# Layer norm of the first tiles by ACT's square root, their transposes inside V, and SwiGLU units ordered by weight columns

## The chip, the cores and the metric

The kernel runs on one core of a Trainium2 chip. Its engines are named as the profile names them: PE (TensorE), DVE (VectorE), ACT (ScalarE), POOL (GpSimd) and SP (SyncE, which here only issues DMAs). The metric is the device time of one execution in microseconds; the median of several runs is compared.

## The reference

One layer norm feeds two branches, linear attention with a Hedgehog feature map and a SwiGLU block, and both are added to the input. All inputs and the output are bfloat16; S = 2048 tokens, D = 640, H = 32 heads of 20, F = 1536.

```python
xn = layernorm(A_x)                       # over the 640 features, eps 1e-5
q, k, v = split(xn @ wqkv)                # (B, H, S, 20) each
pq, pk = q @ w_phi, k @ w_phi             # per head, 20 x 20
phi_q = concat(softmax(pq), softmax(-pq)) # 40 features per head; phi_k likewise
kv = einsum("bhsf,bhsd->bhfd", phi_k, v)
z = einsum("bhsf->bhf", phi_k)
o = einsum("bhqf,bhfd->bhqd", phi_q, kv) / (einsum("bhqf,bhf->bhq", phi_q, z) + 1e-6)
A = o.reshape(B, S, D) @ wo
B = (silu(xn @ w1) * (xn @ w3)) @ w2
out = x + A + B
```

## The kernel before

**Tiles.** The tokens are cut into 16 tiles of 128 (`NST`), and for the SwiGLU products into 4 groups of 512 (`NSC`). D is five chunks of 128 (`KD`), F twelve (`KF`). Each tile is loaded in its natural layout into `xin` (which lies inside `reg_h`), normalised in place, and transposed into `xnT`, whose columns are tokens. Tiles 0 to 3 are transposed by PE through the PSUM tile `pst` and copied out by ACT; tiles 4 to 15 by DMA transposes that SP issues (`x_transposed`, written `T(t)` in the schedule).

**Layer norm.** `ln_stats(t)` is two `bn_stats` and a `bn_aggr` on DVE, which leave mean and variance in `mv`. `ln_pow` is two operations on POOL: the variance plus epsilon (`ve`), and its power of -0.5 (`ry`). `ln_newton` refines that by one Newton step: on DVE for tiles 0 to 3 (two operations, which leave -2 times the value, and ACT multiplies by -0.5 as it copies the transposes out), on POOL for the rest. `ln_x` normalises the tile, on DVE, or on ACT for tiles 12 and 13 (`BY_ACT`).

**Stages.** The work is written out by hand, engine queue by engine queue, and every engine runs its instructions in that order. In the V stage, `V(t)` (`v_unit`, ten matmuls through `by_token`, and two copies by ACT into `vaug`) alternates with `unit()`, one SwiGLU unit. A unit (`glu_unit`) takes 128 columns of w1 and of w3 against 512 tokens: five matmuls for `gp`, five for `up`, a tanh on ACT, and, when the returned function is called (`g0()` and so on), two DVE products into `hT`. `glu` is the list of the 48 units in their order, one token group after the other. Five of them run in the V stage. `FB(d)` (`fuse`) then multiplies w_phi into the k weights, `wkphi`. The phi loop over 16 tiles computes the features of k (`pk`), the sums `kv`, and 31 units; a last loop of 20 turns computes the features of q (`pq`), in its first four turns three units each, from the fifth on the output of one tile per turn (`out_unit`, PSUM tile `acc`).

**PSUM.** Six banks rotate for `pst`, `pv`, `gp`, `up`, `pk`, `pq`, `pf` and `acc`: a matmul into a bank waits until the earlier tile in it has been read.

**Loads.** All DMAs are issued by SP, in order. Two small ACT copies of one element, made after the inverse roots of tile 0 and of tile 1, hold back the loads of tiles 4 and on and of the first SwiGLU weight columns (`ld_glu`). The SwiGLU weights come by columns: 0 to 256 and 256 to 512 early, 512 to 768 in the V stage behind T(9), 768 to 1536 behind it.

```python
T, V = x_transposed, v_unit
...
stats(0, 1)
nc.scalar.copy(out=xin[0:1, 1, 0, 0:1], in_=ry[0:1, 0:1])
ld_tiles(4, 2)
...
lx(0, 1); T(0); warm(4); lx(1, 1); T(1)
V(0); V(1)
stats(2, 1); stats(3, 1)
lx(2, 1); T(2); lx(3, 1); T(3)
...
V(2); V(3)
```

`warm` issues matmuls on zeros, 48 of them before the first transpose.

Of the kernel before, what the change touches and what calls it, by code (L numbers as in the profile page):

```python
# [8 lines left out]
P = 128  # L9
# [3 lines left out]
def kernel(  # L13
# [94 lines left out]
    def ld(dst, src):  # L108
        nc.sync.dma_start(out=dst, in_=src)
# [4 lines left out]
    def ld_glu(f0, f1):  # L114
        for w, src in ((w1, B_w1), (w3, B_w3)):
            ld(w[:, :, f0:f1], src[:, f0:f1].rearrange("(c p) f -> p c f", p=P))

    wps = one.tile([P, KD, Dh], bf, name="wps")
    with tc.manual_schedule():
        def ldT(dst, i, d):  # L120
            rows = slice(d * P, (d + 1) * P)
            nc.sync.dma_start_transpose(
                out=dst[:, :, rows], in_=A_wqkv[rows, i * D : (i + 1) * D]
            )
# [22 lines left out]
        make_identity(nc, ident[:])  # L147
        mhalf = one.tile([P, 4], f32, name="mhalf")
        nc.gpsimd.memset(mhalf[:], -0.5)

        mask = one.tile([P, KD, 8], bf, name="mask")
        nc.gpsimd.memset(mask[:], 1.0)
# [34 lines left out]
        for w in (wkphi, wqphi):  # L187
            nc.gpsimd.memset(w[:, 0, D:FW], 0.0)

        nc.scalar.activation(  # L190
            out=vaug[:, :, :, 20].rearrange("p t h -> p (t h)"),
            in_=ident[:, 0:1].to_broadcast([P, NST * H]), func=AF.Copy, scale=0.0, bias=1.0,
        )


        mv = one.tile([P, NST, 2], f32, name="mv")
        rstd = one.tile([P, NST], f32, name="rstd")

        def ln_stats(t):
            xt = xin[:, (t // 4) % 3, t % 4, :]  # L200
            st = work.tile([P, 2, 6], f32, name="st")
            for i in range(2):
                nc.vector.bn_stats(out=st[:, i, :], in_=xt[:, i * HD : (i + 1) * HD])  # L203
            nc.vector.bn_aggr(out=mv[:, t, :], in_=st[:])  # L204

        ry = one.tile([P, NST], f32, name="ry")
# [3 lines left out]
        def ln_pow(t, n):  # L210
# [3 lines left out]
            )  # L214
            nc.gpsimd.tensor_tensor(out=ry[:, r], in0=ve[:, r], in1=mhalf[:, 0:n], op=ALU.pow)  # L215

        def ln_newton(t, n):


            r = slice(t, t + n)  # L220
            eng = nc.vector if t < BY_DMA else nc.gpsimd
            if n == 1:
                eng.tensor_scalar(
                    out=rstd[:, r], in0=ry[:, r], scalar1=ve[:, r], scalar2=ry[:, r],
                    op0=ALU.mult, op1=ALU.mult,
                )
# [3 lines left out]
            if t < BY_DMA:  # L230
                nc.vector.scalar_tensor_tensor(
                    out=rstd[:, r], in0=rstd[:, r], scalar=-3.0, in1=ry[:, r],
                    op0=ALU.add, op1=ALU.mult,
                )
            else:
                nc.gpsimd.tensor_scalar(
                    out=rstd[:, r], in0=rstd[:, r], scalar1=-0.5, scalar2=1.5,
                    op0=ALU.mult, op1=ALU.add,
                )
                nc.gpsimd.tensor_mul(out=rstd[:, r], in0=rstd[:, r], in1=ry[:, r])  # L240
            if t in BY_ACT:
                nc.gpsimd.tensor_scalar(
                    out=shift[:, r], in0=mv[:, r, 0], scalar1=rstd[:, r], scalar2=-1.0,
                    op0=ALU.mult, op1=ALU.mult,
                )
# [11 lines left out]
                op0=ALU.subtract, op1=ALU.mult,  # L257
            )

        def x_transposed(*ts):  # L260

            for t in ts:
                xn = xin[:, (t // 4) % 3, t % 4, :]
                if t >= BY_DMA:
                    nc.sync.dma_start_transpose(out=xnT[:, :, t * P : (t + 1) * P], in_=xn)
                    continue
                ps = bank("pst", bf)
                for c in range(KD):
                    nc.tensor.transpose(
                        ps[:, c * P : (c + 1) * P], xn[:, c * P : (c + 1) * P], ident[:]  # L270
                    )

                for c0, c1 in ((0, 2), (2, KD)):
                    nc.scalar.mul(
                        out=xnT[:, c0:c1, t * P : (t + 1) * P],
                        in_=ps[:, c0 * P : c1 * P].rearrange("p (c s) -> p c s", s=P),
                        mul=-0.5,
                    )

        def tile_of(t):  # L280
            return slice(t * P, (t + 1) * P)

        def by_token(cols, w, name, cut):


            ps = [bank(name), bank(name)]
            for c in range(KD):
                for i in range(2):
                    a, b = (0, cut) if i == 0 else (cut, w.shape[2] if c == 0 else D)
                    nc.tensor.matmul(  # L290
                        ps[i][:, 0 : b - a],
                        xnT[:, c, cols],
                        w[:, c, a:b],
                        start=(c == 0),
                        stop=(c == KD - 1),
                        skip_group_check=True,
                    )
            return ps

        def v_unit(t, cols=None):  # L300
            ps = by_token(cols or tile_of(t), wv, "pv", HD)
# [252 lines left out]
            )  # L554


        glu = [(sc, fi) for sc in range(NSC) for fi in range(KF)]

        def fill(n):
            for _ in range(n):  # L560
# [2 lines left out]
        def stats(t0, n):  # L563
            for t in range(t0, t0 + n):
                ln_stats(t)
            ln_pow(t0, n)
            if t0 >= BY_DMA:
                ln_newton(t0, n)

        def lx(t0, n):  # L570
            if t0 < BY_DMA:
                ln_newton(t0, n)
            for t in range(t0, t0 + n):
                ln_x(t)

# [12 lines left out]
        def unit():  # L588
            return glu_unit(*glu.pop(0))


        stats(0, 1)
        nc.scalar.copy(out=xin[0:1, 1, 0, 0:1], in_=ry[0:1, 0:1])
        ld_tiles(4, 2)
        ld_tiles(6, 2)
        stats(1, 1)
        nc.scalar.copy(out=w1[0:1, 0, 0:1], in_=ry[0:1, 1:2])
        ld_glu(0, 256)
        ld_tiles(8, 2)
        ld_tiles(10, 2)  # L600
# [75 lines left out]
        for t in range(NST):  # L676
# [7 lines left out]
            fill(1)  # L684
            if t >= 12:
                norm_unit(wkphi, 0, t - 12)
        ld(wo, A_wo.rearrange("(c p) d -> p c d", p=P))

        for t in range(NST + 4):
            if t < NST:
                phi_unit(t, wqphi, "pq")
            if t < 2:
                kv_unit(NST - 2 + t, acc, False, t == 1)
                if t == 1:
                    kv_done(acc)
                    for k in range(0, KF, 4):
                        ld(
                            w2[:, k : k + 4],  # L700
                            B_w2[k * P : (k + 4) * P, :].rearrange("(c p) d -> p c d", p=P),
                        )
# [78 lines left out]
```

## Time and profile before

| | |
|---|---|
| three timed runs | 272.3, 272.51, 273.26 us (median 272.51) |
| profiled execution | 272.0 us, of which the span of the core's instructions is 270.3 us |
| instructions | 5192 |
| busy, share of the span | PE 98%, PE weight loads 61%, DVE 70%, ACT 41%, POOL 36% |
| moved by DMA | 27.80 MB, mean 103 GB/s |
| granted TensorE clock | 1.00 |

Times in the profile are microseconds from the start of the span. A row of a timeline gives start, duration, engine, source line, operation, what it writes and reads with the shapes, and how many instructions the row stands for; in brackets follow the idle time of the engine before it and what ended that. Rows of the groups give busy time and mean nanoseconds of one instead. `reg_h`, `reg_v` and `reg_w` are regions that hold several tiles in turn: an SP row that writes `reg_h` from `in_A_x` is a load of x, one that writes `reg_w` from `in_A_wqkv` a load of attention weights, one that writes `w` a load of SwiGLU weights, and `xnT<-reg_h` a DMA transpose.

### The profile page before, as it was taken

How to read it: one execution, taken by the hardware profiler on the slowest of the kernel's cores; microseconds unless marked ns; L12 is line 12 of the kernel's file. 1: busy time of each engine (PE TensorE's matmuls, PEld its weight loads, DVE VectorE, ACT ScalarE, POOL GpSimd, SP SyncE). 2: the span in 40 equal slices, each digit the busy share in tenths (PEclk: the TensorE clock that was granted, in tenths of full speed). 3: DMA queues.
4: the chain of work that ended last, by engine and by line, in shares of the span. 5: the costliest groups of instructions: out<-in, count | busy, mean ns of one | idle time of the engine just before them, and what ended most of it. 6: DMA issues, size and time to landing. Idle time of an engine off the chain costs nothing.

```text
span 270.3 us, 5192 instructions
## 1 busy us (share of the span) xinstructions
PE 263.7 (98%) x1990; PEld 165.9 (61%) x1990; DVE 189.8 (70%) x349; ACT 109.6 (41%) x258; POOL 97.1 (36%) x104
## 2 busy tenths in 40 slices
PE   7899999999999999999999999999999999999995
PEld 6646576555555555555555455677777777777773
DVE  5999921986677777787768788876766777776341
ACT  6734578344555544455663545422222222221000
POOL 6254720643333333444333321333334444433000
PEclk9999999999999999999999999999999999999999
DMA  7996958940000000000001934346766665576931
GB/s 219 310 246 129 180 117 248 190 122 2 0 0 2 0 2 0 0 5 0 0 2 24 300 75 86 77 109 144 139 136 134 145 130 126 126 144 136 150 101 55
DMA packets 64380, 27.80 MB, mean 103 GB/s; under 512 B 50144, under 2 KB 64352, under 8 KB 64352
## 3 DMA queue, kind: packets, MB, share of 16 engines
q1 hardware_dynamic: 64352, 27.43, 44.9%
q8 instruction: 17, 0.28, 0.4%
q14 instruction: 11, 0.09, 0.1%
HBM read 12.81 MB, written 2.62 MB: 57 GB/s over the span
## 4 chain that ended last, share of the span: by engine, by line
PE 87%; DVE 5%; POOL 3%; DMA 3%; issue 1%; ACT 0%; DVEq 0%
PE acc L505 27%; PE gp L387 17%; PE up L387 17%; PE pq L290 8%; PE pk L290 8%; PE pv L290 4%; DVE st L203 2%; PE pkv L413 2%; PE pr L442 2%; DMA xnT<-reg_h 2%; POOL ry L215 1%; PE pf L371 1%; DVE reg_h L255 1%; DMA reg_h<-in_A_x_dram 1%; DVE mv L204 1%
## 5 line engine op out<-in xcount | busy, mean ns | idle before, releaser
L353 POOL TENSOR_TENSOR phi<-phi,rk 128x1320 bf16<-128x1320 bf16 x32 | 77.2, 2412 | 136.2 <-DVE rk L352 128.4
L350 DVE TENSOR_REDUCE sk<-phi 128x66 f32<-128x1320 bf16 x32 | 48.9, 1529 | 41.2 <-ACT phi L317 40.2
L387 PEld LDWEIGHTS <-w 128*128 128x128 bf16 x480 | 45.5, 97 | 50.7 <-DMA w<-in_B_w_dram 0.3
L387 PE MATMUL up<-xnT,w 128*128 128x512 bf16 x240 | 59.6, 379 | 0.0
L387 PE MATMUL gp<-xnT,w 128*128 128x512 bf16 x240 | 59.6, 379 | 0.0
L290 PEld LDWEIGHTS <-xnT 128*128 128x128 bf16 x480 | 45.5, 97 | 21.7 <-DMA xnT<-reg_h 1.3
L505 PE MATMUL acc<-reg_v,reg_h 128*128 128x320 bf16 (+2 forms) x384 | 54.9, 299 | 0.0
L317 ACT ACTIVATE phi<-pq 128x360 bf16<-128x360 f32 (+1 forms) x64 | 23.3, 451 | 59.2 <-POOL phi L353 53.8
L505 PEld LDWEIGHTS <-reg_h 128*128 128x128 bf16 x384 | 37.3, 98 | 14.5
L395 ACT ACTIVATE th<-gp 128x512 f32<-128x512 f32 x48 | 28.8, 600 | 34.5 <-PE gp L387 30.9
L403 DVE SCALAR_TENSOR_TENSOR reg_h<-gs,up 128x512 bf16<-128x512 bf16 x48 | 33.0, 688 | 5.3 <-PE up L387 0.5
L317 ACT ACTIVATE phi<-pk 128x360 bf16<-128x360 f32 (+1 forms) x64 | 23.3, 451 | 24.5 <-PE pk L290 15.5
L400 DVE SCALAR_TENSOR_TENSOR gs<-th,gp 128x512 bf16<-128x512 f32 x48 | 31.6, 659 | 0.0
L514 DVE TENSOR_TENSOR res<-acc,xr 128x320 bf16<-128x320 f32 (+2 forms) x32 | 14.3, 486 | 21.5 <-PE acc L505 21.5
L290 PE MATMUL pk<-wkphi,xnT 128*128 128x360 bf16 (+2 forms) x160 | 24.7, 300 | 0.0
L290 PE MATMUL pq<-wqphi,xnT 128*128 128x360 bf16 (+2 forms) x160 | 24.6, 300 | 0.0
L505 PE MATMUL acc<-reg_w,reg_v 128*128 128x320 bf16 (+2 forms) x160 | 24.5, 299 | 0.0
L290 PE MATMUL pv<-reg_w,xnT 128*128 128x320 bf16 x160 | 23.0, 299 | 0.5 <-DMA xnT<-reg_h 0.5
L352 DVE RECIPROCAL rk<-sk 128x66 f32<-128x66 f32 x32 | 18.1, 566 | 3.2
L505 PEld LDWEIGHTS <-reg_v 128*128 128x128 bf16 x160 | 15.6, 98 | 6.1
L303 ACT CAST reg_v<-pv 128x320 bf16<-128x320 f32 x32 | 12.1, 430 | 9.7 <-PE pv L290 9.7
L203 DVE BATCH_NORM_STATS2 st<-reg_h 128x6 f32<-128x320 bf16 x32 | 13.6, 467 | 2.1 <-DMA reg_h<-in_A_x_dram 2.1
(62 smaller groups left out, 134.3 us busy)
## 6 DMA issues: line engine op xcount, KB each, us to landing
xr<-in_A_x_dram SPq DMA_DIRECT2D x16, 160.0 KB, 2.5
out_dram<-res SPq DMA_DIRECT2D x15, 160.0 KB, 1.8
reg_h<-in_A_x_dram SPq DMA_DIRECT2D x7, 320.0 KB, 4.9
w<-in_B_w_dram SPq DMA_DIRECT2D x6, 320.0 KB, 5.8
w<-in_B_w_dram SPq DMA_DIRECT2D x2, 960.0 KB, 6.7
reg_v<-in_B_w_dram SPq DMA_DIRECT2D x3, 640.0 KB, 5.9
reg_w<-in_A_wo_dram SPq DMA_DIRECT2D x1, 800.0 KB, 5.3
reg_w<-in_A_wqkv_dram SPq DMA_DIRECT2D x2, 320.0 KB, 4.0
```

The source lines that it names most:

```text
L203: nc.vector.bn_stats(out=st[:, i, :], in_=xt[:, i * HD : (i + 1) * HD])
L290: nc.tensor.matmul(ps[i][:, 0 : b - a], xnT[:, c, cols], w[:, c, a:b], start=(c == 0), stop=(c == KD - 1), skip_group_check=True,)
L317: nc.scalar.activation(out=to[g], in_=p.rearrange("p (c f) -> p c f", f=60), func=AF.Exp, scale=1.0 - 2.0 * g,)
L350: nc.vector.reduce_sum(out=sk[:], in_=rows, axis=AX.X)
L352: nc.vector.reciprocal(out=rk[:], in_=sk[:])
L353: nc.gpsimd.tensor_mul(out=rows, in0=rows, in1=rk[:, :, :, None].to_broadcast([P, 2 * NCH, 3, Dh]))
L387: nc.tensor.matmul(ps[:], w[:, c, fi * P : (fi + 1) * P], xnT[:, c, sc * 512 : (sc + 1) * 512], start=(c == 0), stop=(c == KD - 1),)
L395: nc.scalar.activation(out=th[:], in_=gp[:], func=AF.Tanh, scale=0.5)
L400: nc.vector.scalar_tensor_tensor(out=gs[:], in0=th[:], scalar=1.0, in1=gp[:], op0=ALU.add, op1=ALU.mult)
L403: nc.vector.scalar_tensor_tensor(out=hT[:, 4 * sc : 4 * sc + 4, fi, :], in0=gs[:].rearrange("p (t s) -> p t s", t=4), scalar=0.5, in1=up[: ...
L505: nc.tensor.matmul(ps[:, 0 : b - a], rows[j][0], rows[j][1][:, a:b], start=(j == 0), stop=(j == len(rows) - 1),)
L514: nc.vector.tensor_tensor(out=res[:, a:b], in0=ps[:, 0 : b - a], in1=xr[:, a:b], op=ALU.add)
```

## The change

Tiles 0 to 3 get their inverse root in two steps without POOL: a square root on ACT (`ln_root`, epsilon added as the bias) and a reciprocal on DVE, in place of two POOL operations and two DVE ones. ACT loads the square root's table at the start, and the table for tanh and exp after V(2)'s copies, each by a one-element activation into `table`. The copies that hold loads back move from ACT to POOL. ACT's fill of the ones in `vaug` covers eight tiles instead of sixteen, POOL fills the others.

The transposes of tiles 2 and 3 move into V(1) and V(2), after three of the five chunks, with tile 3's root between the two copies of tile 2's transposes, and tile 2's normalisation between the two halves of tile 3's statistics. ACT copies the transposes without a factor.

The list `glu` is ordered by weight columns: the first four chunks (512 columns) for all four token groups, then the other eight. Six units run in the V stage, the last loop starts with two units instead of three in its first turn. The columns from 512 on are loaded in one piece, behind T(15) and a weight transpose; the load behind T(9) is gone. wo is loaded in two pieces instead of one, w2 in four instead of three.

```diff
+        table = one.tile([P, 1], f32, name="table")
+        nc.scalar.activation(out=table[:], in_=nought[:, 0:1], func=AF.Sqrt)
         nc.scalar.activation(
-            out=vaug[:, :, :, 20].rearrange("p t h -> p (t h)"),
-            in_=ident[:, 0:1].to_broadcast([P, NST * H]), func=AF.Copy, scale=0.0, bias=1.0,
+            out=vaug[:, 0:8, :, 20].rearrange("p t h -> p (t h)"),
+            in_=nought[:, 0:1].to_broadcast([P, 8 * H]), func=AF.Identity, bias=1.0,
         )
+        nc.gpsimd.memset(vaug[:, 8:NST, :, 20], 1.0)
...
-        def ln_stats(t):
+        def ln_stats(t, between=None):
...
             for i in range(2):
                 nc.vector.bn_stats(out=st[:, i, :], in_=xt[:, i * HD : (i + 1) * HD])
+                if i == 0 and between:
+                    between()
...
+        def ln_root(t):
+            r = slice(t, t + 1)
+            nc.scalar.activation(
+                out=ry[:, r], in_=mv[:, t, 1:2], func=AF.Sqrt, bias=eps[:, 0:1], scale=1.0
+            )
...
-        def x_transposed(*ts):
+        def x_transposed(*ts, between=None):
...
                 for c0, c1 in ((0, 2), (2, KD)):
-                    nc.scalar.mul(
+                    nc.scalar.copy(
                         out=xnT[:, c0:c1, t * P : (t + 1) * P],
                         in_=ps[:, c0 * P : c1 * P].rearrange("p (c s) -> p c s", s=P),
-                        mul=-0.5,
                     )
+                    if c0 == 0 and between:
+                        between()
...
-        def by_token(cols, w, name, cut):
+        def by_token(cols, w, name, cut, between=(KD, None)):
             ps = [bank(name), bank(name)]
             for c in range(KD):
+                if c == between[0]:
+                    between[1]()
...
-        glu = [(sc, fi) for sc in range(NSC) for fi in range(KF)]
+        glu = [
+            (sc, fi) for cols in (range(0, 4), range(4, KF)) for sc in range(NSC) for fi in cols
+        ]
...
         def lx(t0, n):
             if t0 < BY_DMA:
-                ln_newton(t0, n)
+                nc.vector.reciprocal(out=rstd[:, t0 : t0 + n], in_=ry[:, t0 : t0 + n])
...
-        stats(0, 1)
-        nc.scalar.copy(out=xin[0:1, 1, 0, 0:1], in_=ry[0:1, 0:1])
+        ln_stats(0)
+        ln_root(0)
+        nc.gpsimd.tensor_copy(out=xin[0:1, 1, 0, 0:1], in_=ry[0:1, 0:1])
...
         lx(1, 1)
         T(1)
+        ln_stats(2)
+        ln_root(2)
         V(0)
-        V(1)
-        stats(2, 1)
-        stats(3, 1)
-        lx(2, 1)
-        T(2)
+        def third():
+            T(2, between=lambda: ln_root(3))
+        ln_stats(3, between=lambda: lx(2, 1))
+        V(1, between=(3, third))
         lx(3, 1)
-        T(3)
+        V(2, between=(3, lambda: T(3)))
+        nc.scalar.activation(out=table[:], in_=nought[:, 0:1], func=AF.Tanh)
...
-        V(2)
         V(3)
...
         g2 = unit()
         g1()
+        lx(8, 1)
+        T(8)
+        g3 = unit()
+        g2()
+        lx(9, 1)
+        T(9)
+        ldT(wkT, 1, 2)
         V(4)
         V(5)
-        g2()
+        stats(10, 2)
+        g3()
         V(6)
-        lx(8, 1)
-        T(8)
-        lx(9, 1)
-        T(9)
-        ld_glu(512, 768)
-        ldT(wkT, 1, 2)
         V(7)
-        stats(10, 2)
-        g3 = unit()
         stats(12, 1)
-        stats(13, 1)
+        g4 = unit()
         lx(10, 2)
         T(10, 11)
+        stats(13, 1)
         V(8)
-        g3()
+        g4()
         stats(14, 2)
         lx(12, 1)
         T(12)
         V(9)
-        g4 = unit()
+        g5 = unit()
         lx(13, 1)
         T(13)
         ldT(wkT, 1, 3)
         V(10)
         phi_blocks()
-        g4()
+        g5()
         lx(14, 2)
         T(14, 15)
         ldT(wkT, 1, 4)
         V(11)
-        ld_glu(768, F)
+        ld_glu(512, F)
...
             if t < 4:
-                fill(3)
+                fill(3 if t else 2)
```

More of the change, by code (lines that the diff above doesn't have):

```diff
@@ L149 @@
         nc.gpsimd.memset(mhalf[:], -0.5)
+        eps = one.tile([P, 1], f32, name="eps")
+        nc.gpsimd.memset(eps[:], EPS)
         mask = one.tile([P, KD, 8], bf, name="mask")
@@ L215, in ln_pow @@
             nc.gpsimd.tensor_tensor(out=ry[:, r], in0=ve[:, r], in1=mhalf[:, 0:n], op=ALU.pow)
+        def ln_root(t):
[3 more added lines that the diff above has]
+            )
         def ln_newton(t, n):
             r = slice(t, t + n)
-            eng = nc.vector if t < BY_DMA else nc.gpsimd
+            eng = nc.gpsimd
             if n == 1:
@@ L229, in ln_newton @@
                 eng.tensor_mul(out=rstd[:, r], in0=rstd[:, r], in1=ve[:, r])
[L230 to L240, printed above, removed]
+            eng.tensor_scalar(
+                out=rstd[:, r], in0=rstd[:, r], scalar1=-0.5, scalar2=1.5,
+                op0=ALU.mult, op1=ALU.add,
+            )
+            eng.tensor_mul(out=rstd[:, r], in0=rstd[:, r], in1=ry[:, r])
             if t in BY_ACT:
-                nc.gpsimd.tensor_scalar(
+                eng.tensor_scalar(
                     out=shift[:, r], in0=mv[:, r, 0], scalar1=rstd[:, r], scalar2=-1.0,
@@ L298, in by_token, with v_unit @@
             return ps
-        def v_unit(t, cols=None):
-            ps = by_token(cols or tile_of(t), wv, "pv", HD)
+        def v_unit(t, cols=None, between=(KD, None)):
+            ps = by_token(cols or tile_of(t), wv, "pv", HD, between)
             for i in range(2):
@@ L566, in stats @@
             ln_pow(t0, n)
-            if t0 >= BY_DMA:
-                ln_newton(t0, n)
+            ln_newton(t0, n)
         def lx(t0, n):
             if t0 < BY_DMA:
-                ln_newton(t0, n)
+                nc.vector.reciprocal(out=rstd[:, t0 : t0 + n], in_=ry[:, t0 : t0 + n])
             for t in range(t0, t0 + n):
@@ L589, in unit @@
             return glu_unit(*glu.pop(0))
-        stats(0, 1)
-        nc.scalar.copy(out=xin[0:1, 1, 0, 0:1], in_=ry[0:1, 0:1])
+        ln_stats(0)
+        ln_root(0)
+        nc.gpsimd.tensor_copy(out=xin[0:1, 1, 0, 0:1], in_=ry[0:1, 0:1])
         ld_tiles(4, 2)
         ld_tiles(6, 2)
-        stats(1, 1)
-        nc.scalar.copy(out=w1[0:1, 0, 0:1], in_=ry[0:1, 1:2])
+        ln_stats(1)
+        ln_root(1)
+        nc.gpsimd.tensor_copy(out=w1[0:1, 0, 0:1], in_=ry[0:1, 1:2])
         ld_glu(0, 256)
@@ L686 @@
                 norm_unit(wkphi, 0, t - 12)
-        ld(wo, A_wo.rearrange("(c p) d -> p c d", p=P))
+        for c0, c1 in ((0, 3), (3, KD)):
+            src = A_wo[c0 * P : c1 * P, :]
+            ld(wo[:, c0:c1], src.rearrange("(c p) d -> p c d", p=P))
         for t in range(NST + 4):
@@ L697 @@
                     kv_done(acc)
-                    for k in range(0, KF, 4):
+                    for k in range(0, KF, 3):
                         ld(
-                            w2[:, k : k + 4],
-                            B_w2[k * P : (k + 4) * P, :].rearrange("(c p) d -> p c d", p=P),
+                            w2[:, k : k + 3],
+                            B_w2[k * P : (k + 3) * P, :].rearrange("(c p) d -> p c d", p=P),
                         )
             if t < 4:
-                fill(3)
+                fill(3 if t else 2)
             else:
```

## The prediction

> **What bounds the kernel now.** I read the page's shares first, then busy time by stage, TensorE's waits, and the timelines of the stage in which TensorE waits. The stages:
>
> ```profile
> span 270.3 us, 5192 instructions
> PE 263.7 (98%) x1990; PEld 165.9 (61%) x1990; DVE 189.8 (70%) x349; ACT 109.6 (41%) x258; POOL 97.1 (36%) x104
> ...
> 14.30:20.70 6.40, 6.40 (x31) 2.79 (x30) 5.91 (x16) 2.55 (x5) 3.42 (x14) 1.00 1.13 231
> 20.70:26.10 5.40, 5.40 (x41) 3.91 (x41) 5.04 (x13) 2.27 (x6) 2.33 (x8) 1.00 0.64 124
> 26.10:33.80 7.70, 7.25 (x42) 3.83 (x40) 7.19 (x19) 4.42 (x10) 5.97 (x19) 1.00 1.01 177
> ...
> 43.70:267.10 223.40, 223.40 (x1679) 138.56 (x1676) 158.80 (x266) 83.51 (x201) 77.18 (x32) 1.00 0.38 86
> ```
>
> The columns after the stretch are its length, then busy time of PE, weight loads, DVE, ACT, POOL, then the granted clock (full everywhere). From 43.7 to 267.1 us PE is never free. A change in the first 43.7 us therefore moves the end one for one, and it can win only time in which PE waits there. The timeline of PE and the queue of SP, which issues the DMAs:
>
> ```profile
> 6.21 0.45 PE L269 MATMUL pst<-ident,reg_h 128*128 128x128 bf16 x5 [0.95 <-POOL ry L215]
> 7.23 0.45 PE L269 MATMUL pst<-ident,reg_h 128*128 128x128 bf16 x5 [0.34 <-DVE reg_h L255]
> 7.52 2.88 PE L290 MATMUL pv<-reg_w,xnT 128*128 128x320 bf16 x20
> 11.24 0.45 PE L269 MATMUL pst<-ident,reg_h 128*128 128x128 bf16 x5 [0.56 <-DVE reg_h L255]
> 14.25 1.24 PE L387 MATMUL gp<-xnT,w 128*128 128x512 bf16 x5
> 18.56 1.24 PE L387 MATMUL gp<-xnT,w 128*128 128x512 bf16 x5
> 33.82 4.25 PE L290 MATMUL pv<-reg_w,xnT 128*128 128x320 bf16 x30 [0.47 <-DMA xnT<-reg_h]
> 43.56 1.65 PE L290 MATMUL pk<-wkphi,xnT 128*128 128x360 bf16 x10
> 26.39 1.14 SPq L109 DMA_DIRECT2D w<-in_B_w_dram  x2
> 28.90 6.89 SPq L265 DMA_TRANSPOSE xnT<-reg_h  x4
> 28.90 4.87 DMA xnT<-reg_h
> 38.70 1.36 PE pv L290 x10
> ```
>
> Two losses are to be seen. The first SwiGLU unit starts only at 14.25, because the transposes of tiles 0 to 3 wait for the layer norm on DVE and POOL. And V(10) at 33.82 waits for the DMA transpose of tile 10, issued at 28.90 and 4.87 us under way behind two weight loads of 26.39. The last two rows are from the chain of waits. A SwiGLU unit lasts 2.16 (two from 14.25 to 18.56), a V 1.36 (ten matmuls, last row), and a fuse 0.32: 33.82 to 43.56 holds six V and five fuses.
>
> **Part 1, the start.** The rows of DVE and ACT that price it:
>
> ```profile
> 4.98 0.21 DVE L204 BATCH_NORM_AGGREGATE mv<-st 128x2 f32<-128x12 f32 x1
> 5.21 0.27 DVE L223 TENSOR_SCALAR rstd<-ry,ve 128x1 f32<-128x1 f32 x1
> 5.51 0.16 DVE L231 SCALAR_TENSOR_TENSOR rstd<-rstd,ry 128x1 f32<-128x1 f32 x1
> 5.71 0.45 DVE L255 TENSOR_SCALAR reg_h<-reg_h,mv,rstd 128x640 bf16<-128x640 bf16 x1
> 11.10 0.88 DVE L203 BATCH_NORM_STATS2 st<-reg_h 128x6 f32<-128x320 bf16 x2
> 12.14 0.83 DVE L203 BATCH_NORM_STATS2 st<-reg_h 128x6 f32<-128x320 bf16 x2
> L593 ACT CAST reg_h<-ry 1x1 bf16<-1x1 f32 x1 | 0.2, 193 | 0.6 <-POOL ry L215 0.6
> L250 ACT ACTIVATE reg_h<-reg_h,shift,rstd 128x640 bf16<-128x640 bf16 x2 | 1.8, 920 | 0.9 <-POOL shift L242 0.9
> L395 ACT ACTIVATE th<-gp 128x512 f32<-128x512 f32 x48 | 28.8, 600 | 34.5 <-PE gp L387 30.9
> L352 DVE RECIPROCAL rk<-sk 128x66 f32<-128x66 f32 x32 | 18.1, 566 | 3.2
> L274 ACT ACTIVATE xnT<-pst 128x256 bf16<-128x256 bf16 x4 | 1.6, 388 | 0.5 <-PE pst L269 0.5
> 2.09 2.48 ACT L190 ACTIVATE reg_v<-ident 128x512 bf16<-128x512 bf16 x1
> 2.66 0.47 SPq L109 DMA_DIRECT2D reg_h<-in_A_x_dram  x1
> DMA to landing us min/median/max: 4.0/4.0/4.0
> 3.18 0.47 SPq L109 DMA_DIRECT2D reg_w<-in_A_wqkv_dram  x1
> DMA to landing us min/median/max: 4.4/4.4/4.4
> ```
>
> Under each of the two loads stands its landing time, from the view of its tile cut to that load alone.
>
> The square root of 128x1 isn't in the trace. It costs no less than the 1x1 CAST (0.19). From above: L250 with two per-partition operands takes 920 ns for 640 elements, L395 with none 600 for 512; nearly all of the gap of 320 could be operands, some 0.11 to 0.16 each, and one such operand on 0.19 gives 0.30 to 0.35. I take 0.28. The reciprocal of 128x1 lies between L231's 0.16 and L223's 0.27; L352 spends 566 ns on 66 elements, so one element is nearly all fixed cost: 0.17. ACT's fill before it is halved from 2.48; even unhalved it ends near 4.8, before DVE is free at 5.2, so it costs nothing. POOL's half stands ahead only of the two gate copies, and the loads behind those have until 10.6.
>
> Step by step: DVE still finishes the statistics of tiles 0 and 1 before the first normalisation, so the earlier root only saves one of two small operations. Reciprocal 5.15, normalisation 5.35 to 5.80, T(0) at 5.82 (was 6.21). Tile 1: T(1) at 6.39 (was 7.23). V(0) at 6.72, when ACT's first copy of T(0) is done, and 8.08 to V(1). The weight load that V(0)'s fourth chunk needs was issued at 3.18 and took 4.4: there by about 7.55, wanted at 7.53. Tile 2's statistics start when its load (2.66, and 4.0) lands, near 6.68: root 7.88 to 8.16, reciprocal, normalised by 8.85. V(1)'s first three chunks end at 8.90, so T(2) at 8.92 fits, and V(1) ends at 9.75. V(2) follows T(2)'s first copy (0.39) at 9.81; its third chunk waits for the second copy at 10.42, as the root of tile 3 (0.28) stands between the copies on ACT. T(3) at 10.72, V(2)'s rest, V(3) 11.61 to 12.97. The first unit starts at **12.97 instead of 14.25: 1.28 won**. With 0.35 and 0.27 it is 13.25, with the small ends 12.9.
>
> **Part 2, ACT's second table.** A load of a table is seen once:
>
> ```profile
> L190 ACT ACT_TABLE_LOAD x1 | 1.3, 1283 | 0.8 <-PEq L765 0.8
> 15.46 0.80 DVE L255 TENSOR_SCALAR reg_h<-reg_h,mv,rstd 128x640 bf16<-128x640 bf16 x2 [0.26 <-POOL rstd L240]
> 16.19 0.67 DVE L400 SCALAR_TENSOR_TENSOR gs<-th,gp 128x512 bf16<-128x512 f32 x1
> 16.96 0.69 DVE L403 SCALAR_TENSOR_TENSOR reg_h<-gs,up 128x512 bf16<-128x512 bf16 x1
> ```
>
> The new one stands behind V(2)'s copies, 12.51 to 13.79, then its dummy to 14.07. Queued behind it are V(3)'s copies (ready at 12.97, now 14.04) and unit 0's tanh, now 14.7 to 15.3. DVE wants that tanh at 15.66, behind tiles 4 and 5: covered by 0.4 us, cost nothing. This is the place where a rule speaks against the change: the Trainium skill, "ScalarE: Activation LUTs", section "What ACT_TABLE_LOAD costs", puts a switch of sets at 1283 ns of load and 1380 ns of drain, 2.66 us, and says to batch by set. By that price the saving would shrink by an estimated 1.0 us. The trace shows the load's 1283, but at an empty engine, and an activation 0.01 us behind it; a drain in mid-stream no row here shows.
>
> **Part 3, the V stage.** Six units instead of five run before the phi loop; the sixth's 2.15 leaves the end of the loop (fill(2) for fill(3)), so PE's total work is unchanged. It moves V(10) to 34.36, and the two weight loads of 26.39 are gone from in front of T(10). DVE reaches T(10)'s normalisation at 27.8, SP issues it near 28.4; even 4.87 us land it by 33.3. **The 0.47 wait goes.** What is late next is DVE. From 10.57 it has, up to unit 3's first product, eight tiles of statistics at 1.03 (11.10 to 12.14), six normalisations at 0.36 (two from 15.46 to 16.19), three units at 1.39 (0.77 from 16.19 to 16.96, and 0.6 to the next) and 0.2 of waits for POOL: 14.8 us, then the product's own 0.67, to 26.08. In the program as built, V(7)'s second half reuses the PSUM bank that this product frees. PE is there at 12.97 + 4 x 2.16 + 3 x 1.36 + 0.14 (one matmul) = 25.83: **a new wait of 0.27**. Between nothing and 0.5 (DVE 2% either way). The last transposes: unit 5 starts at 32.2, its gate is done at 33.45, its tanh takes 0.6 and ACT's normalisation of tile 13 behind it 0.92, to 34.9; SP then issues T(13), one weight transpose, T(14) and T(15) 1.3 apart (6.89 for four, a wait within), T(14) at 37.63.
>
> ```profile
> DMA to landing us min/median/max: 2.6/2.6/2.6
> w<-in_B_w_dram SPq DMA_DIRECT2D x2, 960.0 KB, 6.7
> ```
>
> The first row is that of the last three transposes of before, from 34.6 on: T(14) lands at 40.23. V(14) wants it three V, two fuses, one V and a fuse after V(10): 40.79. Covered by 0.56, at nothing; the weight transpose behind T(15), at 42.87, by 0.97. The columns from 512 on now come in one load behind these, a third larger than the 6.7 us ones; the first unit that needs them is the 17th, in the phi loop's sixth turn near 72 us, with the load over by some 53. Split loads of wo and w2 add two issues on SP in a stretch where PE has no wait. All this at nothing.
>
> **Sum.** 1.28 + 0.47 - 0.27 = 1.48, rounded 1.5 of the profiled execution's 272.0 (span 270.3, 1.7 around it): 270.5. The three timed runs lie at 272.3 to 273.26, median 272.51, half a microsecond above the profiled one; against them the same saving gives **271.0**, and all figures below are on that footing. About 0.5%, 1.36 us, is what a measurement of this kernel can tell from no change, so the forecast lies just beyond it.
>
> **Rivals.**
> The transposes fall behind (the slow side). SP's queue from T(13) to the last weight transpose is serial; if each landed after 4.87, as T(10) did, and issued 0.3 later each, T(14) would land at 43.1, 2.3 behind V(14), the last fuse 0.25 more: 271.0 + 2.55 = 273.55, slower than before. It begins to cost at a landing above 3.2 and eats the whole gain at 4.7. For it: T(10)'s row. Against: that had weight loads in front, now gone, and 2.6/2.6/2.6.
> ACT held 2.6 us by the table (twice its row, the engine emptying first). V(3)'s copies and the tanh come 1.3 later, 0.85 more than is covered; DVE passes it on, and V(4), V(5), V(7) wait for banks, 1.3 in all instead of 0.27: 272.0. The 0.01 us between load and first activation of before speaks against it. It is the case in which the Trainium skill's price of a switch, of part 2, holds.
> DVE sets the stage. At 5% more than my sum of 14.8 unit 3's product is 0.75 later: V(7) waits 1.0, 271.75. For it: DVE is busy 5.04 to 7.19 us of each stretch of 5.4 to 7.7 there. Against: it has waits for POOL within these, which a late DVE would fill.
> The start doesn't deliver. The DMA gate now opens 0.6 earlier, so loads of tiles 4 to 7 run beside the last V weights; landing 0.5 later than 7.54 delays V(0) by as much: 271.5. Against: the same queue, issued in order.
> More than forecast: no V(7) wait, small ends for root and reciprocal, 270.4.
>
> **Chances.** As forecast 0.58 (270.6 to 271.4; 0.44 of it beyond 0.5%), more 0.14, ACT 0.06, DVE 0.08, weights 0.05, transposes 0.09 (0.07 over 0.5%, with the weight transposes as late). Faster 0.44 + 0.14 = 0.58; slower 0.07; within 0.5% the rest, 0.35. Range 270.0 to 272.4: it leaves out the transposes and little below.
>
> **What would show it.** T(0) near 5.8, the first gp near 13.0, no wait at V(10), a short wait of PE for gs within V(7), the first pk near 44.2 (43.56 + 2.15 - 1.5), 224.6 from there to the end (270.3 - 43.56 - 2.15). A first gp after 13.6 or waits over 0.8 us between it and pk make it wrong; so does a PE wait after 45.

## The result, and the profile after

The changed kernel takes **271.27 us** (median of six runs, 270.84 to 272.32) where the kernel before takes 272.50 (six runs): ratio 0.9948, interval 0.9924 to 0.9972. In two later comparisons the same file gave 271.38 against 272.61 (0.9958, 0.9942 to 0.9973) and 271.41 against 272.64 (0.9954, 0.9936 to 0.9971). Each time 1.23 us lie between the medians; 1.5 were forecast.

The profiled execution of the changed kernel is the slowest of the six runs (272.32, span 270.5). So the same file was profiled twice more, `a2_after` (270.88, span 269.1) and `a3_after` (271.20, span 269.5), and the kernel before once more, `b2_before` (272.27, span 270.6). The page and TensorE's timeline of the first:

```profile
span 270.5 us, 5193 instructions
PE 264.7 (98%) x1990; PEld 166.6 (62%) x1990; DVE 188.5 (70%) x345; ACT 110.1 (41%) x263; POOL 95.7 (35%) x100
...
5.79 0.45 PE L278 MATMUL pst<-ident,reg_h 128*128 128x128 bf16 x5
6.35 0.45 PE L278 MATMUL pst<-ident,reg_h 128*128 128x128 bf16 x5
6.71 1.22 PE L301 MATMUL pv<-reg_w,xnT 128*128 128x320 bf16 x6
9.05 1.52 PE L301 MATMUL pv<-reg_w,xnT 128*128 128x320 bf16 x10 [1.12 <-DMA reg_w<-in_A_wqkv_dram]
10.40 0.44 PE L278 MATMUL pst<-ident,reg_h 128*128 128x128 bf16 x5
12.19 0.45 PE L278 MATMUL pst<-ident,reg_h 128*128 128x128 bf16 x5
14.47 1.24 PE L398 MATMUL gp<-xnT,w 128*128 128x512 bf16 x5
27.75 1.38 PE L301 MATMUL pv<-reg_w,xnT 128*128 128x320 bf16 x9 [0.24 <-DVE gs L411]
45.73 1.65 PE L301 MATMUL pk<-wkphi,xnT 128*128 128x360 bf16 x10
```

and the same of `a2_after`:

```profile
span 269.1 us, 5193 instructions
...
5.84 0.45 PE L278 MATMUL pst<-ident,reg_h 128*128 128x128 bf16 x5
6.40 0.45 PE L278 MATMUL pst<-ident,reg_h 128*128 128x128 bf16 x5
6.76 2.55 PE L301 MATMUL pv<-reg_w,xnT 128*128 128x320 bf16 x16
9.15 0.44 PE L278 MATMUL pst<-ident,reg_h 128*128 128x128 bf16 x5
13.21 1.24 PE L398 MATMUL gp<-xnT,w 128*128 128x512 bf16 x5
26.50 1.38 PE L301 MATMUL pv<-reg_w,xnT 128*128 128x320 bf16 x9 [0.24 <-DVE gs L411]
44.48 1.65 PE L301 MATMUL pk<-wkphi,xnT 128*128 128x360 bf16 x10
```

Read each in three stretches. Up to T(1) they agree with one another and with the forecast. From the first gp to the first pk both take 31.26 or 31.27 us (before: 29.31, and one unit of 2.15 less in it). From pk to the end they take 224.8 and 224.6. The difference between these two executions of one file lies between V(0) and the first gp. What comes later there shows in DVE's timeline, at the statistics of tile 2, the first that need the load of tiles 2 and 3: of the two executions above, and of the second of the kernel before.

```profile
8.13 0.89 DVE L210 BATCH_NORM_STATS2 st<-reg_h 128x6 f32<-128x320 bf16 x2 [1.83 <-DMA reg_h<-in_A_x_dram]
```
```profile
6.90 0.89 DVE L210 BATCH_NORM_STATS2 st<-reg_h 128x6 f32<-128x320 bf16 x2 [0.56 <-DMA reg_h<-in_A_x_dram]
```
```profile
7.43 0.89 DVE L203 BATCH_NORM_STATS2 st<-reg_h 128x6 f32<-128x320 bf16 x2 [0.24 <-DMA reg_h<-in_A_x_dram]
```

The view of the tile, cut to that one load, gives its landing: 5.4 us after its issue in the first of these, 4.2 in the second; 4.7 in `b2_before`, 4.0 in the first profile of the kernel before.

```profile
L109 SPq DMA_DIRECT2D reg_h<-in_A_x_dram x1: 469/469/469, 2.7 to 2.7; - x1
DMA to landing us min/median/max: 5.4/5.4/5.4
```
```profile
DMA to landing us min/median/max: 4.2/4.2/4.2
```

### The profile page after: what moved, and what is told of

It reads as the page before. It is cut to its first block, busy times and chain, and to the rows that moved or that the text cites. A ratio compares the mean times of both kernels' runs of the same rounds, so it can differ in the third digit from the quotient of the medians.

```text
span 270.5 us, 5193 instructions
## 1 busy us (share of the span) xinstructions
PE 264.7 (98%) x1990; PEld 166.6 (62%) x1990; DVE 188.5 (70%) x345; ACT 110.1 (41%) x263; POOL 95.7 (35%) x100
## 4 chain that ended last, share of the span: by engine, by line
PE 89%; DVE 4%; DMA 2%; POOL 2%; issue 1%; SPq 1%; ACT 0%; DVEq 0%
PE acc L516 27%; PE gp L398 18%; PE up L398 18%; PE pq L301 8%; PE pk L301 8%; PE pv L301 5%; DMA reg_w<-in_A_wqkv_dram 2%; PE pkv L424 2%; PE pr L453 2%; DVE st L210 1%; PE pf L382 1%; SPq L109 1%; DVE reg_h L264 1%; POOL ry L224 1%; DVE gs L411 0%
## 5 line engine op out<-in xcount | busy, mean ns | idle before, releaser
L301 PE MATMUL pv<-reg_w,xnT 128*128 128x320 bf16 x160 | 23.9, 299 | 1.4 <-DMA reg_w<-in_A_wqkv_dram 1.1
```

Of the source, the lines that this page charges most:

```text
L301: nc.tensor.matmul(ps[i][:, 0 : b - a], xnT[:, c, cols], w[:, c, a:b], start=(c == 0), stop=(c == KD - 1), skip_group_check=True,)
```

## The experiments

The theory to be tested: the start wins about 1, as far as the landing of the first loads lets it, and hands part of that on to unit 3's gate product at V(7), while the order of the units takes V(10)'s wait away. The rivals were the earlier gate of the loads, the v weights at V(0), and the zeros in front of T(0). Ratios below are against the kernel before in the same comparison. The kernel before, `e1_root` and `e8_order` have five units ahead of the first pk, all others six, 2.15 us more.

| kernel | median us | ratio, interval | first gp, first pk |
|---|---|---|---|
| before (profile 1; `b2_before`) | 272.50 to 272.64; 272.83 | 1; 1.0000 (0.9981 to 1.0019) | 14.25, 43.56; 14.59, 43.83 |
| changed (profile 1; `a2_after`; `a3_after`) | 271.27; 271.38; 271.41 | 0.9948; 0.9958; 0.9954 | 14.47, 45.73; 13.21, 44.48; 13.38, 44.64 |
| `e1_root` | 272.61 | 1.0007 (0.9992 to 1.0022) | 13.93, 43.87 |
| `e2_units` | 271.70 | 0.9965 (0.9951 to 0.9979) | 14.29, 45.12 |
| `e8_order` | 272.17 | 0.9972 (0.9955 to 0.9989) | 14.30, 43.30 |
| `e3_gate` | 271.20 | 0.9945 (0.9931 to 0.9959) | 14.03, 45.27 |
| `e4_weights` | 271.11 | 0.9948 (0.9935 to 0.9961) | 13.27, 44.50 |
| `e5_warm` | 271.12 | 0.9947 (0.9929 to 0.9965) | 13.22, 44.45 |
| `e6_queue` | 271.64 | 0.9960 (0.9944 to 0.9976) | 14.51, 45.77 |
| `e7_g3` | 271.00 | 0.9943 (0.9926 to 0.9960) | 13.70, 44.76 |
| `e9_both` | 270.88 | 0.9925 (0.9899 to 0.9951) | 13.30, 44.32 |

**The root alone, `e1_root`.** Square root, reciprocal, ACT's tables, fills, gates and the split loads of wo and w2 as changed, on the kernel before; T(2) and T(3) stay between V(1) and V(2), the units as before.

```diff
-        stats(0, 1)
-        nc.scalar.copy(out=xin[0:1, 1, 0, 0:1], in_=ry[0:1, 0:1])
+        ln_stats(0)
+        ln_root(0)
+        nc.gpsimd.tensor_copy(out=xin[0:1, 1, 0, 0:1], in_=ry[0:1, 0:1])
...
+        ln_stats(2)
+        ln_root(2)
         V(0)
+        ln_stats(3)
+        ln_root(3)
         V(1)
```

> The start alone: square root by ACT, reciprocal by DVE, copies that gate the loads on POOL; the transposes of tiles 2 and 3 stay behind V(1), five units, units and loads in the old order. My theory: it brings T(0) to 5.8 and the first gp to 13.3 where the V weights land by 7.6 us, 0.9 us less than before (271.6); where they land at 9.0, as in the profile of the changed kernel, only 0.2 or so are left (272.3). Rival (the start was covered anyway, only the order of the units counts): 272.5.

No gain, neither the 0.9 nor the 0.2 of the theory: 272.61 is the rival's number. TensorE's timeline and the landing of T(10), issued at 29.3:

```profile
6.14 0.72 PE L278 MATMUL pst<-ident,reg_h 128*128 128x128 bf16 x5
34.13 4.25 PE L301 MATMUL pv<-reg_w,xnT 128*128 128x320 bf16 x30 [0.87 <-DMA xnT<-reg_h]
```
```profile
L274 SPq DMA_TRANSPOSE xnT<-reg_h x1: 1217/1217/1217, 29.3 to 29.3; - x1
DMA to landing us min/median/max: 4.8/4.8/4.8
```

The first gp, at 13.93, is 0.32 earlier instead of the 0.9 expected: T(0) comes only at 6.14, and T(2) stands behind all of V(1). T(10) is issued 0.36 later than before, right behind two loads and a weight transpose in SP's queue, and V(10) waits 0.87 instead of 0.47. Another 0.21 is lost in front of V(4), where no row names a wait. So pk comes 0.31 later than before: what this start wins is lost again by V(10), and as much again.

**The units alone, `e2_units`.** The kernel before with the new list of units, six of them in the V stage, and the columns from 512 on in one load behind T(15).

```diff
-        glu = [(sc, fi) for sc in range(NSC) for fi in range(KF)]
+        glu = [
+            (sc, fi) for cols in (range(0, 4), range(4, KF)) for sc in range(NSC) for fi in cols
+        ]
...
-                fill(3)
+                fill(3 if t else 2)
```

> The units alone: columns first, six units in the V stage, one load of the columns from 512 on behind the last transpose; the layer norm of tiles 0 to 3 and their transposes as before. My theory: the wait of 0.47 at V(10) goes and no new one at V(7) comes, since PE is 1.3 later there than in the changed kernel: 272.0. Rival (DVE sets the stage): the wait at V(7) stands here too, 272.3 to 272.5.

```profile
22.93 5.60 PE L290 MATMUL pv<-reg_w,xnT 128*128 128x320 bf16 x40
35.39 4.24 PE L290 MATMUL pv<-reg_w,xnT 128*128 128x320 bf16 x30
```
```profile
L265 SPq DMA_TRANSPOSE xnT<-reg_h x1: 1201/1201/1201, 28.9 to 28.9; - x1
DMA to landing us min/median/max: 4.5/4.5/4.5
```

Four V in one piece: V(7) waits for nothing here, since PE comes later than DVE. V(10) waits for nothing either, although T(10) still took 4.5 us. From gp to pk it is 45.12 - 14.29 = 30.83, less the unit of 2.15 28.68: 0.63 shorter than before, of which the wait's own row shows 0.47. The rest is not in that row: from the last matmul in front of V(10) to its first, start to start, the trace of before has 0.63 more than between a unit and a V without a wait. The median gives 0.91, the interval 0.6 to 1.3; the profile explains the lower part of that, the rest stays open.

**Order without the sixth unit, `e8_order`.** The list of units and the one load behind T(15), but five units at their old places.

```diff
-        ld_glu(512, 768)
...
-        ld_glu(768, F)
+        ld_glu(512, F)
```

> The kernel before with the units ordered by weight columns and the columns from 512 on loaded in one piece behind T(15); five units in the V stage, at their old places. So no weight load stands in front of T(10), but V(10) comes no later. Theory: T(10)'s wait is made by the two loads in front of it; without them it is issued by 28.3 and lands by 32.8, V(10) at 33.35 waits for nothing, 0.5 to 0.9 us faster than before, like the units alone. Rival: T(10) takes 4.5 us without those loads too (33.46 less 28.93 with the units alone), and it is the sixth unit that covers it: V(10) still waits 0.1 to 0.5, 0 to 0.4 faster.

```profile
33.40 4.24 PE L290 MATMUL pv<-reg_w,xnT 128*128 128x320 bf16 x30
39.47 0.48 PE L371 MATMUL pf<-wphi,reg_w 128*128 128x140 bf16 x6
39.95 1.53 PE L290 MATMUL pv<-reg_w,xnT 128*128 128x320 bf16 x10
```
```profile
L265 SPq DMA_TRANSPOSE xnT<-reg_h x1: 1200/1200/1200, 28.9 to 28.9; - x1
DMA to landing us min/median/max: 2.6/2.6/2.6
```

T(10) is issued at 28.9 as ever, but lands in 2.6, and V(10) starts at 33.40 without a wait. The median is 0.47 less than before. The fourteen profiles bear the theory out: behind the two weight loads T(10) took 4.8 to 4.9 us in all three (kernel before twice, `e1_root`), without them 2.6 to 4.5 in the other eleven. It isn't quite safe without the sixth unit: with the 4.5 of `e2_units` T(10) would land at 33.4, just when V(10) wants it, and the V at 39.95 starts 0.48 behind the start of the fuse in front of it, where the next one has 0.31 (41.32 to 41.63). From gp to pk 29.00: 0.31 saved; with the sixth unit, which moves every V behind it, it is 0.63.

**The gate, `e3_gate`.** The changed kernel, with the loads of tiles 4 to 7 held until the root of tile 1.

```diff
-        nc.gpsimd.tensor_copy(out=xin[0:1, 1, 0, 0:1], in_=ry[0:1, 0:1])
-        ld_tiles(4, 2)
-        ld_tiles(6, 2)
         ln_stats(1)
         ln_root(1)
+        nc.gpsimd.tensor_copy(out=xin[0:1, 1, 0, 0:1], in_=ry[0:1, 1:2])
+        ld_tiles(4, 2)
+        ld_tiles(6, 2)
```

> The changed kernel with the loads of tiles 4 to 7 held until the root of tile 1 (issue near 5.9 instead of 4.9). If the earlier gate made the V weights land late: they land near 7.5 again, the first gp is at 13.0 and the time 0.5 to 1.5 us below the changed kernel's. If the landing varies from execution to execution whatever the gate: the same time within 0.2 us, and a landing between 7.5 and 9.

```profile
8.61 1.52 PE L301 MATMUL pv<-reg_w,xnT 128*128 128x320 bf16 x10 [1.07 <-DMA reg_w<-in_A_wqkv_dram]
```

The weights are late with the later gate too: the load of tiles 2 and 3 took 5.0 here, and 4.7 in `b2_before`, whose gate is the old one. The ratio, 0.9945, is that of the changed kernel, 0.9948. A late landing does not need the earlier gate; it varies from execution to execution (4.2 to 5.4 in eight profiles with the gate of the change, 4.0 to 4.7 in four with that of before). Whether the gate adds a little on average, so few profiles can't tell.

**The v weights, `e4_weights`.** The changed kernel, which leaves out the later v weights in V(0), so that tile 0's v is not the reference's.

```diff
-                        w[:, c, a:b],
+                        w[:, 0 if near else c, a:b],
...
-            ps = by_token(cols or tile_of(t), wv, "pv", HD, between)
+            ps = by_token(cols or tile_of(t), wv, "pv", HD, between, cols is None and t == 0)
```

> The changed kernel with V(0) multiplying all five chunks by the first chunk's weights (tile 0's v is another number), so that V(0) waits for no late weight. If the V weights' landing is what the start waits for: V(0) runs through from 6.7 us, V(1) then waits for them at 8.1 at most, and the time is up to 0.9 us below the changed kernel's where they are late, the same where they are in time. If the load of tiles 2 and 3 is what counts: T(2) stays as late and the time is the same.

```profile
6.75 2.35 PE L301 MATMUL pv<-reg_w,xnT 128*128 128x320 bf16 x16
9.20 0.45 PE L278 MATMUL pst<-ident,reg_h 128*128 128x128 bf16 x5
```

V(0) waits for nothing (its row takes 2.35 us, 2.55 in `a2_after`), T(2) still stands at 9.20, and the ratio over six runs, 0.9948, is that of the changed kernel. V(0)'s wait of 1.12, TensorE's longest in the first profile, costs next to nothing: what TensorE gains there it would lose in front of T(2).

What sets T(2), and with it the first gp, is tile 2. In nine profiles with the changed order of the start, DVE's statistics of tile 2 begin at 6.88 to 8.23 us (`after` 8.13, `a2_after` 6.90, `a3_after` 7.04, `e3_gate` 7.71, `e4_weights` 7.00, `e5_warm` 6.88, `e6_queue` 8.23, `e7_g3` 7.37, `e9_both` 6.99), each time released by the load. The first gp follows **6.27 to 6.34 us** behind in all nine. In the order of before it follows 7.16 behind (14.25 less 7.09, where DVE had no wait, and 14.59 less 7.43).

That alone does not tell tile 2 from the v weights, since on one queue the last of these land 0.9 us behind tiles 2 and 3 in every profile (issued 0.5 later, they take 5.8 where tiles 2 and 3 take 5.4, and 4.6 where these take 4.2). Two runs tell them apart: in `e4_weights` and in `e6_queue` below, V(0) runs through without a late weight, and T(2) comes 2.20 behind the start of tile 2's statistics. In the other seven it comes 2.25 to 2.28 behind. The late v weights therefore cost at most 0.08 beyond what tile 2 costs.

**Fewer zeros, `e5_warm`.** `WARM = 42` instead of 48.

> The changed kernel with 42 instead of 48 matmuls on zeros before the first transpose. Theory: TensorE reaches full speed at a moment that varies, so the 48 end between 5.3 and 6.4 us, and in some executions T(0) waits for them and not for DVE; six fewer take 0.34 to 0.64 us off that queue, T(0) stands near 5.8 in every execution, and the time is 0 to 0.3 us below the changed kernel's. Rival: the queue is idle time that DVE covers, and fewer matmuls on zeros leave TensorE slower at T(0) and V(0): the same to 0.5 us slower. If neither acts, the weights that V(0) waits for set the start anyway: same.

271.12 against 271.38 of the changed kernel in the same comparison; the intervals overlap. T(0) stands at 5.84 with 42 as with 48. That the queue of zeros can matter is seen in `e1_root`: the 32 zeros from 2.73 on lasted 3.62 us there and 2.99 in `a2_after`, and T(0) came at 6.14. But slow matmuls can also reach as far as T(0): in `e9_both`, with 42, its five took 0.69 us instead of 0.45, and T(1) came 0.18 later than in `a2_after`. That is not the price of fewer zeros alone, as T(0) took 0.72 in `e1_root` with 48 (above) and 0.46 in `e5_warm` with 42.

```profile
5.83 0.69 PE L278 MATMUL pst<-ident,reg_h 128*128 128x128 bf16 x5
6.58 0.44 PE L278 MATMUL pst<-ident,reg_h 128*128 128x128 bf16 x5
```

The Trainium skill, "TensorE: Matmul & The Clock Gate", "Part 1: The HAM clock gate", says that the step to full speed hangs on a free-running window of some 3.4 us and not on a number of matmuls, and so varies between runs. These rows agree with it as far as they go: 42 or 48 doesn't decide how fast T(0) is. That it was the clock is not shown, since the granted clock reads 1.00 in these stretches too. Whether 42 is better stays open.

**Another queue for the v weights, `e6_queue`.**

```diff
-            ld(wv[:, c : c + n], src.rearrange("(c p) f -> p c f", p=P))
+            nc.scalar.dma_start(out=wv[:, c : c + n], in_=src.rearrange("(c p) f -> p c f", p=P))
```

> The changed kernel with the three loads of the v weights issued by ACT, first on its queue, instead of by SP behind the loads of x. Theory: V(0) waits up to 1.1 us for the last of these loads, and they are late because they stand fourth to sixth on one queue, 0.5 us apart; issued some 1 us earlier they land by 7.5, V(0) waits for nothing, and the first gp starts near 13.0: 0.3 to 1.0 us below the changed kernel. Rival: the DMA engines share out a fixed rate in these us, so that the weights take it from x; tile 0 lands later than 3.1, and tiles 2 and 3 later than 8: the same, or up to 1 us slower.

The rival held. (On SP's queue the three loads stand third, fourth and sixth.) Tile 0, issued as before, lands in 3.1 us instead of 2.3, and everything behind it moves; the median is 0.26 above the changed kernel's in the same comparison. DVE's timeline, T(2) on TensorE, and the landing of tile 0's load:

```profile
3.88 0.89 DVE L210 BATCH_NORM_STATS2 st<-reg_h 128x6 f32<-128x320 bf16 x2 [2.89 <-DMA reg_h<-in_A_x_dram]
8.23 0.89 DVE L210 BATCH_NORM_STATS2 st<-reg_h 128x6 f32<-128x320 bf16 x2 [0.97 <-DMA reg_h<-in_A_x_dram]
10.43 0.45 PE L278 MATMUL pst<-ident,reg_h 128*128 128x128 bf16 x5 [0.40 <-DVE reg_h L264]
```
```profile
DMA to landing us min/median/max: 3.1/3.1/3.1
```

The Trainium skill, "DMA: Bandwidth & Descriptors", "Queues, rings and completion order", says that each DMA engine takes turns between the queues that have work for it, packet by packet. The trace agrees: tile 0 stood first on its queue both times, and it took 0.8 longer once other loads came by a second one.

**Unit 3's products first, `e7_g3`.**

```diff
-        stats(10, 2)
+        ln_stats(10)
         g3()
+        ln_stats(11)
+        ln_pow(10, 2)
+        ln_newton(10, 2)
```

> The changed kernel with unit 3's two products on DVE between the statistics of tile 10 and of tile 11, not behind both. Theory: the wait of 0.24 us in V(7) is for that gate product; it comes 1.03 us earlier, the wait goes, and T(10) comes at most 0.1 later than it did, covered by 1 us at V(10): 0.2 us faster. Rival: PE then waits for the same 0.24 at V(10) or for another bank: same. Statistics of tile 11 late behind the products: the two POOL steps and T(10) 1.4 later, V(10) waits up to 0.5: slower by 0.3.

No row names a wait in V(7) any more, V(10) at 35.04 has none either, and from gp to pk it is 44.76 - 13.70 = 31.06, 0.2 less. DVE's rows show the two products, the gate product 1.76 us earlier than in the first profile after, in an execution that started 0.77 earlier:

```profile
22.74 5.43 PE L301 MATMUL pv<-reg_w,xnT 128*128 128x320 bf16 x37
```
```profile
25.31 0.63 DVE L411 SCALAR_TENSOR_TENSOR gs<-th,gp 128x512 bf16<-128x512 f32 x1
26.04 0.69 DVE L414 SCALAR_TENSOR_TENSOR reg_h<-gs,up 128x512 bf16<-128x512 bf16 x1
```

Half of the loss is still there. In `a2_after` V(7)'s second matmul starts 0.54 behind its first, where 0.14 is usual; here it is 0.34 (26.45 to 26.79), and it starts 0.06 behind the end of the second product, at 26.73. That it now waits for that product is likely, not shown.

The median, 271.00 against 271.38, fits, but the intervals overlap; what is shown is the 0.2 in the profile.

**Three more profiles.**

> The changed kernel once more, on the same chip as the three others, so that they can be compared with it: 271.2 (270.8 to 271.6). Theory: its start varies between executions with the landing of the v weights and of tiles 2 and 3; another profile shows another landing (7.5 to 9.0 us for the last chunks of the weights), and its first gp is the landing's lateness behind 13.0, by at most 1.5. Rival: the landing is set by the changed kernel's earlier gate, then it stands at 9.0 again and the first gp at 14.4.

> The changed kernel for comparison, 271.2 to 271.4; first gp between 13.2 and 14.5 by when the last v weights land, a wait of 0.24 in V(7) in each case.

> The kernel before, 272.6. Theory: its profiled execution of 272.0 was one of its fastest; in an execution near the median V(10) waits more than 0.47, up to 0.9, or the first gp starts later than 14.25, up to 14.7. Rival: V(10)'s wait is 0.47 again and what varies lies behind pk: more than 226.74 us from the first pk to the end.

`a3_after` has its first gp at 13.38 and its first pk at 44.64. In `b2_before` V(10) waits 0.39, so the wait of before is not larger in other executions; what is later there is the first gp, 14.59, because tiles 2 and 3 landed later than DVE was ready for them (the 0.24 above). Behind pk it takes 226.8, against 226.7.

**The two together, `e9_both`.** 42 zeros and unit 3's products first.

> The changed kernel with 42 matmuls on zeros and with unit 3's products ahead of the statistics of tile 11: 270.8 to 271.0, 0.2 to 0.4 below the changed kernel in the same runs, if the two add up; 271.1 to 271.2 if the start's varying landing hides them.

270.88 against 271.41 of the changed kernel in the same comparison, with 31.02 from gp to pk: the fastest version seen. Its interval against the kernel before, 0.9899 to 0.9951, overlaps that of the changed kernel, 0.9936 to 0.9971, so the half microsecond between the two is likely, not settled.

## Why the prediction was right, and where it was off

**The operations.** The square root took 0.29 (forecast 0.28), the reciprocal 0.11 to 0.16 (0.17). T(0) came at 5.79, 5.84 and 5.96 in the three profiles (5.82), T(1) at 6.35, 6.40 and 6.47 (6.39).

**The start: the term that was mis-sized.** The step that failed is "tile 2's statistics start when its load lands, near 6.68". The landing of 4.0 us was taken from one profile as if it were the load's price. It was 4.2 and 5.4 after, and 4.7 in the second profile of before. The order that the prediction worked out is right to 0.05: from the statistics to the first gp it says 12.97 - 6.68 = 6.29, and nine profiles show 6.27 to 6.34. Before, DVE came to tile 2 only at 7.09, and a landing at 6.7 or at 7.0 was the same to it. The change takes that slack away and starts at the landing itself. By these rows it shortens the way from tile 2's statistics to the first gp by 7.16 - 6.31 = 0.85; a landing ahead of 7.09 adds what it is early, 0.4 at the forecast's 6.68. With the landing of `a2_after` the start is worth 14.25 - 13.21 = 1.04, with that of `a3_after` 0.87; 1.28 was forecast.

The rival "the start doesn't deliver" had its finger on the landing, but on the wrong load and the wrong cause: the v weights' wait costs at most 0.08 (`e4_weights`, `e6_queue`), and the landing is late without the earlier gate too (`e3_gate`). In the first profile after, the first gp stands at 14.47, past the 13.6 that was to make the forecast wrong; that execution shows the step failing by its full size, the others by 0.24 and 0.41.

**ACT's second table.** ACT's timeline in the first profile after, and below it DVE's first gate product:

```profile
13.31 0.78 ACT L314 CAST reg_v<-pv 128x320 bf16<-128x320 f32 x2
14.11 1.28 ACT L634 ACT_TABLE_LOAD   x1
15.40 0.20 ACT L634 ACTIVATE table<-nought 128x1 f32<-128x1 bf16 x1
15.51 0.74 ACT L314 CAST reg_v<-pv 128x320 bf16<-128x320 f32 x2
16.14 0.61 ACT L406 ACTIVATE th<-gp 128x512 f32<-128x512 f32 x1
17.17 0.68 DVE L411 SCALAR_TENSOR_TENSOR gs<-th,gp 128x512 bf16<-128x512 f32 x1
```

The load follows 0.02 behind the last cast and is followed 0.01 later, in mid-stream, with casts in front and behind. The tanh ends at 16.75, DVE takes it at 17.17, without a wait, behind tiles 4 and 5: covered by 0.4, as forecast. The 1380 ns of drain that the Trainium skill, "ScalarE: Activation LUTs", "What ACT_TABLE_LOAD costs", adds to a switch are not seen here; the measurement decides, and the rival that rests on it is out.

**The V stage.** V(10)'s wait is gone. The new one in V(7) is 0.24 by its row in all three profiles, for the product that was named (0.27; the forecast's own terms, 10.57 + 14.8 + 0.67, give 26.04 instead of 26.08, and 0.21). `e7_g3`, which moves unit 3's two products alone, takes 0.2 off the stage. The stretch from gp to pk was to be 44.2 - 12.97 = 31.2 and is 31.3. That it fits so well is luck in part: V(10)'s wait was worth 0.63 and not 0.47 (`e2_units`), and V(7) costs 0.43 and not 0.27 (31.26 against the 30.83 of `e2_units`). The first was read off the row's idle time, the second worked out; each is 0.16 short, and the two errors cancel. Behind pk 224.6 were forecast; 224.8, 224.6 and 224.9 were measured. The transposes T(13) to T(15) and the weights behind them are late in no profile: PE has no wait between V(7) and pk.

**The sum.** By the profile the start's 0.9 to 1.0 and the V stage's 29.31 + 2.15 - 31.26 = 0.2 make 1.1 to 1.2; the medians show 1.23. That sum leaves out the first profile after and `b2_before`: over all pairs of profiles, pk less the sixth unit comes between 0.0 later and 1.5 earlier. The forecast of 1.5 lies inside all three intervals of the ratio, so the medians alone don't refute it; what the profiles show is a first gp 0.24 to 0.41 later than forecast, or 1.50 in the first profile after, as tiles 2 and 3 land later than in the one profile that it went by.

**What each part is worth.** The root alone brings nothing. The units alone bring 0.91 by the medians and 0.6 by the profile, both parts together 1.23 and 1.1 to 1.2. So of the 0.9 to 1.0 by which the first gp comes earlier, some half is left at the end: the earlier start makes V(7)'s wait, and the V stage of `e2_units` is 0.43 shorter than that of the changed kernel. By the medians the start adds 0.3 to the units, with overlapping intervals. The whole start, with T(2) and T(3) inside V but the old order of units, was not run.

## What to carry to other kernels

When a change moves an engine up to the moment at which a load lands, the landing's spread becomes the kernel's: look at two or three executions before taking a landing time as a term, and at what slack stood in front of it. The longest wait of a page can be free; ask what the engine would have waited for next, and put the price on the chain that ends last. A gain at the start has to be followed through every later wait: here a wait at V(10) swallowed one of 0.3, and a wait at V(7) takes 0.4 of the larger one. And when two landings always come the same distance apart, no number of profiles tells which of them matters; a run that moves one of them does.

## What was not expected of the hardware

The same load, issued at 2.66 us behind the same four others, landed between 4.0 and 5.4 us later in executions of nearly the same program. The DMA transpose of tile 10 took 4.8 to 4.9 us with two weight loads in front of it and 2.6 to 4.5 without, 3.6 to 4.1 in three executions of the changed kernel alone. What spreads either stays open. A wait costs more than its row says: the 0.47 at V(10) cost 0.63 between gp and pk, the 0.24 at V(7) 0.40 from one matmul to the next, and in V(7) of `e7_g3` 0.20 went by with no wait named at all. Not tried: tiles 2 and 3 loaded ahead of the v weights on the one queue. Whether it would pay is open, since V(0) already comes within 0.08 of holding T(2) back, and its weights would then land later.
